# A gated delta-rule attention feeding a GELU layer on one core: the same instructions in another written-out order

## The chip, the core and the metric

The kernel runs on one core of a Trainium2 chip. A core has a matrix engine (TensorE, in the profile PE, with its weight loads as PEld), a vector engine (DVE), a scalar engine (ACT), GpSimd (POOL) and a sync engine (SP) that here only starts transfers. Each engine works through its own queue in order, and semaphores between the engines are the only thing that holds one queue back for another. The metric is the device time of one execution in microseconds (us).

## The reference

Two stages follow each other. The first is a recurrence over 768 steps for each of 4 x 8 heads of width 48, the second a plain two-layer network with a tanh-GELU:

```python
k_n = k / (norm(k) + 1e-6)
for t in range(S):                        # S = 768; state is 48 x 48 for each batch and head
    y[t]  = q[t] @ state
    v_old = state^T @ k_n[t]
    state = state + beta[t] * outer(k_n[t], v[t] - v_old)
x = y.transpose(0, 2, 1, 3).reshape(3072, 384)
h = x @ w_in                              # 384 x 2048
out = gelu_tanh(h) @ w_out                # 2048 x 384
```

## The kernel before, in words

The 768 steps are cut into 12 chunks of 64. Inside a chunk the recurrence becomes products of matrices: the triangular system that couples the 64 steps is inverted by five doubling steps, and only the 48 x 48 state is carried from chunk to chunk. The 32 heads are handled as 2 units of work per chunk (unit u belongs to chunk u // 2), so there are 24 units.

One unit is prepared like this (`prep`). `kc`, `kb` and `qb` bring k, scaled k and q into bf16; `Tc`, `Tb`, `Tk`, `Tq` or `T` transpose them on PE and `kT...` copies the result out of PSUM (from unit 6 on, some transposes are transfers, `turn`). `GM`, `GQ`, `G2` and `G` are the products k k^T and k q^T on PE; `ln`, `wpm`, `wpq` and `wp` copy them out under a triangular mask on DVE (line 527). `X10` and `X11` put the diagonal in (line 557 on POOL, 559 on DVE). Then come the doubling steps i = 1 to 5: a product `A{i}` on PE, `rt{i}` on DVE, which adds twice the identity while it copies out of PSUM (line 580), a product `B{i}` on PE, and a copy back into the block-diagonal operand, `bde{i}0` and `bde{i}1` (line 325, on ACT or DVE) or `bdf` (lines 325 and 331) or `xi` with two `bdc` (line 610). The next step waits for that copy. For a step there are two other forms: `J{i}` and `C{i}` on PE with a plain copy `rj{i}` on ACT or DVE in place of `A{i}` and `rt{i}`; and in the first units `wqa` (a plain copy on ACT) with `wqb` (the mask, on POOL) in place of `wpq`.

`chain` then carries the state over a chunk: `K`, `R`, `U`, `Un`, `S`, `Sn`, `Q`, `O`, `On`, and `X` with `xT`, which hands the chunk to the network. `mlp` is the network: sixteen products `up0` to `up15` on PE (line 717), four `gelu` on ACT (line 721), eight groups `down` on PE (line 728), two copies `Z` and the transfers `out`.

`norms` makes the scale for k: `sq`, `sum`, `pow`, `eps`, `nsq` or `nsa`, `inv`, `ib`. The root of the first three chunks is taken on ACT (`pow` after `tabS`, which loads the table of the root, line 349); `tabG` (line 752) loads the table of the GELU. `warm_up` offers 70 products of zeros, `fill` (line 387), whose result nobody reads; as many of them run as the order names.

The order of all this is written out by hand in a string, `ORDER`: a list of some 1,700 names, each with its engine (`:a` ACT, `:d` DVE, `:g` POOL, `:s` SP; no letter where only one engine is possible) and, for products, its PSUM bank. `Flow.order` puts each name into the queue of its engine in that sequence, and `Flow.emit` adds the semaphore waits that the data and the banks need. Transfers are in the list too: they are issued by SP, ACT or (for the weights) POOL, at the place in that engine's queue where the list names them. q, k and v have three buffers each (chunk modulo 3).

Of the kernel before, what the change touches and what calls it, by code (L numbers as in the profile page):

```python
# [19 lines left out]
betaN000 betaN001 betaN010 betaN011 k1.01:s epsb:d k1.10:a fill45@2 beta11:a k1.11:s fill22@1 beta10:s sq.0b:g tabS pow.0a eps.0a:d twob:d J1.1@3 sum.0b  # L20
q0.1:s mup1 nsa.0a v0.11:s inv.0a ib.0a:d upone0 v0.10:s pow.0b fill55@2 q0.0:a eps.0b:d nsa.0b sq.1:d fill36@0 kb.0:d kc.1:a bdz1:g k2.10:s fill49@2 inv.0b
ib.0b:g kb.1:g betaT1@0 kc.0:a Tc.1@1 fill9@2 betaA111 betaA110 betaA101 sum.1 pow.1 eps.1:g nsq.1:g kTc.1:d q1.1:s fill60@4 Tb.0@2 kTb.0:d Tc.0@4 kTc.0:d
Tb.1@1 inv.1 triwpm0:d betaA100 ib.1:d GM.0@6 ln.0 kb.3:g v1.11:a v0.01:s X11.0:g wpm.0 kTb.1:a GM.1@4 ln.1 X10.0:g v0.00:a qb.0:a Tq.0@1 wpm.1 kc.3:a Tk.3@2
triln3:a A1.0@0 X10.1:d kTq.0:d GQ.0@4 k2.00:a kTk.3:a q1.0:a X11.1:g C1.1 rj1.1:a rt1.0 B1.0@0 k2.01:s pad2:d kb.2:d wpq.0 bde10.0:a kc.2:d GM.3@6 ln.3
B1.1@1 bde10.1:d bde11.0:a A2.0@0 rt2.0 bde11.1:a A2.1@1 rt2.1 Tk.2@3 triwpm2:a B2.0@2 B2.1@0 qb.1:a v1.00:s Tq.1@1 v1.10:s v1.01:s wpm.3 bde21.0:d k2.11:s
sq.2:a sum.2 bde20.0:a A3.0@2 fill1@4 fill4@5 fill42@4 fill14@5 q2.0:s bdf20.1:a bdf21.1:d A3.1@0 rt3.0 B3.0@2 kTk.2:a GM.2@4 rt3.1 triln2:a ln.2 w2.1 qb.2:a
bdz4:g bdz3:g X10.3:g kTq.1:a X11.3:g w1.1 A1.3@0 pad5:g pow.2 B3.1@1 k3.10:s GQ.1@6 wpm.2 rt1.3 kc.5:a k4.10:s q2.1:s bdf30.0:a bdf31.0:a A4.0@2 rt4.0 vs.1:g
B1.3@0 R0b.0:g bdf30.1:a bdf31.1:a A4.1@1 bdz2:g wpq.1 v2.00:s bdf10.3:a qb.3:g eps.2:g B4.0@2 bde41.0:a nsq.2:g bde40.0:a X11.2:g rt4.1 q3.0:s X10.2:g A1.2@4
rt1.2 B4.1@1 bde41.1:d w1.0 bde40.1:a Tq.2@3 kTq.2:d B1.2@4 bde10.2:a triwpm4:g A5.0@5 rt5.0 A5.1@1 rt5.1 bde11.2:a bdf11.3:d k3.01:s B5.0@2 bde50.0:a A2.2@3
rt2.2 B5.1@4 bde50.1:d bde51.0:a k3.00:s bde51.1:a B2.2@0 bde21.2:a bde20.2:a inv.2 A2.3@1 rt2.3 R0a.0:g U.0@4 Un.0:d B2.3@1 A3.2@0 rt3.2 q4.0:s Tq.3@2 O.0@4  # L30
On.0:d fill6@3 bde21.3:a qb.5:g B3.2@0 bde20.3:a A3.3@1 rt3.3 kTq.3:a GQ.3@6 X.0@2 xT.0:d B3.3@1 triwpm5:g bdf30.2:a bdf31.2:a A4.2@0 rt4.2 bdf30.3:a
bdf31.3:d up4.0@2 up12.0@4 up13.0 k3.11:s wpq.3 ib.2:g kb.5:g B4.2@0 up5.0 up6.0 up7.0 up14.0 A4.3@1 up15.0 up0.0@6 q3.1:s tabG bde41.2:d bde40.2:a up1.0
up2.0 A5.2@0 rt4.3 gelu1.0 pad4:g kb.4:g kc.7:a up3.0 B4.3@1 w2.0 kc.4:g sq.3:g sum.3 k4.00:s k5.10:s q4.1:s gelu3.0 gelu0.0 qb.4:g T.4@2 kT.4:a T.5@4 rt5.2
bde41.3:d bde40.3:d kT.5:d pow.3 eps.3:g up8.0@6 up9.0 v2.11:s A5.3@0 rt5.3 k5.00:a G2.5@2 ln.5 bdz5:g kc.6:g X11.5:g k4.01:a G2.4@4 S.0@0 Sn.0:a ln.4 X11.4:g
X10.4:g G.4@2 wp.4 up10.0 qb.9:a up11.0 gelu2.0 nsq.3:g qb.6:g qb.7:g k4.11:s K.1@0 X10.5:g v2.10:s G.5@4 down00.0@2 B5.3@3 wp.5 A1.4@6 bde51.3:a inv.3
down01.0 down10.0@7 k5.11:s rt1.4 v2.01:s q5.0:s v3.01:s ib.3:g k5.01:s R.1 B1.4@6 B5.2@4 down02.0 sq.4:a A1.5@5 down11.0 bdf10.4:a sum.4 GQ.2@0 q5.1:s
bdf50.2:a kb.7:g bdf11.4:a bde50.3:d A2.4@3 q6.0:s bdf51.2:a turn.7 rt1.5 kb.6:g v4.01:a pow.4 eps.4:g B1.5@6 nsq.4:g rt2.4 U.1@4 bde11.5:a qb.11:g kc.9:g
Un.1:a wpq.2 down12.0 B2.4@3 Q.1@0 kc.10:d S.1@4 bde10.5:a bde20.4:d inv.4 O.1 Sn.1 bde21.4:a J2.5@6 On.1:a C2.5 A3.4@3 rt3.4 turn.6 down13.0 rj2.5:a X.1@0
ib.4:d B3.4@5 B2.5@4 qb.8:g sq.5:a xi3.4:a kb.9:g fill27@6 down03.0 xT.1:d bdc30.4:g up0.1@0 sum.5 up1.1 v3.10:a bdc31.4:g up2.1 bdf20.5:a q6.1:s A4.4@5
# [4 lines left out]
nsq.5:g v4.00:a rt2.6 k6.00:s k6.10:s turn.9 R.2 B2.6@6 xi5.5:a bdc50.5:d A2.7@2 kc.11:g bdc51.5:g inv.5 xi2.6:a down00.1@3 gelu3.1 rt2.7 q7.1:a bdc21.6:g
bdc20.6:d U.2@4 B2.7@2 Un.2:a bde21.7:a down12.1 A3.6@6 bde20.7:d Q.2@0 rt3.6 v4.10:s ib.5:g sq.7:g G2.8@4 v3.00:s O.2 ln.8 sq.6:g X11.8:g X10.8:g A3.7@2
down01.1 B3.6@6 S.2@4 sum.7 On.2:a G.8@0 down02.1 rt3.7 Sn.2 bdf30.6:a bdf31.6:a kb.10:g kb.11:g v5.11:s B3.7@2 wp.8 bdf30.7:a A4.6@6 v3.11:s q8.1:a rt4.6
down03.1 bdf31.7:a turnx.2 q7.0:a down13.1 A1.8@0 A4.7@6 turn.10 B4.6@1 G2.9@4 Z0.1:a pow.7 v5.00:s rt1.8 Z1.1:a xi4.6:a v4.11:s G.9@2 bdc41.6:g rt4.7
# [8 lines left out]
A2.10@0 K.4@6 Z1.2:d rt2.10 bdf41.9:a up2.3 up3.3 B1.11@3 v6.01:a G2.12@0 A5.9@2 gelu0.3 R.4 k9.01:a up8.3@6 qb.14:g bde10.11:a bdc50.8:g bde11.11:a v7.00:s
kc.16:g up9.3 B2.10@4 rt5.9 v7.11:a B5.9@5 ln.12 up10.3 inv.7 up4.3@0 bdc51.8:g X11.12:g A2.11@3 xi5.9:d bdc51.9:g bde20.10:a bde21.10:a up5.3 sum.8 out11.2:a
up6.3 up7.3 A3.10@2 rt2.11 up11.3 bdc50.9:g U.4@4 down10.3@3 rt3.10 B2.11@2 gelu1.3 Un.4:d Q.4@0 G2.13@4 gelu2.3 v7.10:s bdf20.11:a G.12@6 O.4 bdf21.11:a
ln.13 down11.3 A3.11@2 On.4:a v6.11:a B3.10@5 G.13@0 wp.12 pow.8 X11.13:g rt3.11 bdf30.10:a eps.8:g S.4@6 down00.3@4 X10.12:g v6.10:a down01.3 bdf31.10:d Sn.4
# [732 lines left out]
```

## Time and profile before

| | |
|---|---|
| time, median of 3 runs | 260.44 us (260.43 to 261.03) |
| the profiled execution | 259.31 us, of which 257.6 us are the span from the first to the last instruction |
| busy in the span | PE 242.8 us (94%), DVE 209.1 us (81%), ACT 185.4 us (72%), POOL 137.7 us (53%) |
| mean granted clock of PE | 0.98 |
| transfers | 31.46 MB in 116,788 packets, mean 122 GB/s |

Busy times are those of the profiled execution. A transfer that an engine issues is not counted as busy time of that engine; such rows carry a q behind the engine's name (SPq, ACTq, POOLq), and their duration is the time that issuing took. In a row of the timeline the first number is the start in us, the second the duration; what stands in brackets at its end is the time that the engine sat idle before it and what it waited for. Durations of PE are modelled and overlap, so that eight products can show 0.6 us and the next eight start after 0.3 us.

### The profile page before, as it was taken

What the parts mean: (1) busy time and instruction counts of PE and PEld (TensorE: products, weight loads), DVE (VectorE), ACT (ScalarE), POOL (GpSimd) and SP (SyncE); (2) the same over time, 40 slices, a digit from 0 to 9 for tenths busy, and PEclk for the clock granted to TensorE, in tenths of its full rate; (3) what the DMA queues carried; (4) which work ended last, traced back from release to release, by engine and by line L of the source; (5) the groups of instructions that cost most, each with busy time, mean ns of one, the idle gap of its engine ahead of it and who ended that gap; (6) DMA issues with size and microseconds to landing.
All of it is one profiled execution on the core that took longest, in us unless ns stands there. A gap on an engine that the chain in (4) does not pass through costs nothing.

```text
span 257.6 us, 12254 instructions
## 1 busy us (share of the span) xinstructions
PE 242.8 (94%) x5491; PEld 190.4 (74%) x5491; DVE 209.1 (81%) x363; ACT 185.4 (72%) x295; POOL 137.7 (53%) x206
## 2 busy tenths in 40 slices
PE   7878789999999989999999999999999999999994
PEld 2466569677877868977877887778877878878772
DVE  6898998999989779999999899789887889575000
ACT  0679989688978868966967876977856766665252
POOL 4488666995989918763576786536370330240000
PEclk9965999999999999999999999999999999999999
DMA  5999999999968965948959359247867031011322
GB/s 90 199 193 195 202 193 191 167 198 128 173 122 171 191 103 98 147 98 157 185 109 193 67 114 181 45 93 110 147 96 142 3 64 36 30 36 33 64 61 61
DMA packets 116788, 31.46 MB, mean 122 GB/s; under 512 B 110848, under 2 KB 115968, under 8 KB 116736
## 3 DMA queue, kind: packets, MB, share of 16 engines
q1 hardware_dynamic: 84448, 19.82, 46.9%
q10 hardware_dynamic: 29408, 7.72, 16.1%
q0 software_dynamic: 2880, 3.15, 7.6%
q8 instruction: 43, 0.70, 1.1%
q14 instruction: 9, 0.07, 0.1%
HBM read 20.64 MB, written 4.72 MB: 98 GB/s over the span
## 4 chain that ended last, share of the span: by engine, by line
PE 82%; DVE 12%; ACTq 2%; ACT 2%; issue 1%
PE ps L728 24%; PE ps L717 24%; PE ps L568 21%; PE ps L523 4%; PE ps L640 3%; DVE bd L325 2%; DVE rt L580 2%; PE ps L663 2%; DVE wp L527 2%; ACTq L425 2%; DVE ln L527 2%; PE ps L688 1%; PE ps L675 1%; DVE kT L325 1%; PE ps L387 1%
## 5 line engine op out<-in xcount | busy, mean ns | idle before, releaser
L717 PE MATMUL ps<-xT,W 128*128 128x256 bf16 x576 | 77.6, 273 | 0.0
L325 ACT ACTIVATE bd<-ps 64x512 bf16<-64x512 f32 x110 | 62.8, 588 | 19.2 <-PE ps L568 17.8
L728 PE MATMUL ps<-W,gT 128*128 128x384 bf16 x384 | 74.2, 326 | 0.0
L721 ACT ACTIVATE gT<-ps 128x1024 bf16<-128x1024 f32 x48 | 48.8, 1020 | 19.1 <-PE ps L717 18.1
L717 PEld LDWEIGHTS ps<-xT,W 128*128 128x128 bf16 x576 | 50.5, 98 | 6.8
L580 DVE TENSOR_TENSOR rt<-ps,two 128x512 bf16<-128x512 f32 x70 | 47.2, 683 | 6.6 <-PE ps L568 6.0
L728 PEld LDWEIGHTS ps<-W,gT 128*128 128x128 bf16 x384 | 33.2, 98 | 16.6 <-ACT gT L721 0.2
L610 POOL COPY bd<-xi 64x256 f32<-64x256 f32 x45 | 19.3, 429 | 46.9 <-ACT xi L325 25.7
L557 POOL TENSOR_SCALAR_AFFINE_SELECT bd<-ln 64x512 bf16<-64x512 bf16 x42 | 28.3, 674 | 14.9 <-DVE ln L527 10.2
L527 DVE CAST_PREDICATED wp<-mup,ps 128x1024 bf16<-128x1024 uint16 (+1 forms) x28 | 29.7, 1065 | 1.4 <-PE ps L523 1.1
L568 PE MATMUL ps<-rt,bd 128*128 128x64 bf16 x576 | 28.5, 196 | 1.5 <-DVE rt L580 1.5
L568 PE MATMUL ps<-wp,bd 128*128 128x64 bf16 (+1 forms) x576 | 28.3, 190 | 1.7 <-DVE ob L325 0.6
L568 PEld LDWEIGHTS ps<-wp,bd 128*128 128x128 bf16 x576 | 23.4, 99 | 6.7 <-DVE ob L325 1.0
L568 PEld LDWEIGHTS ps<-rt,bd 128*128 128x128 bf16 x576 | 23.8, 100 | 5.8 <-DVE rt L580 2.3
L451 POOL TENSOR_TENSOR nrm<-nrm,half 128x16 f32<-128x16 f32 x9 | 26.2, 2908 | 3.2 <-DVE nrm L449 3.0
L580 DVE TENSOR_TENSOR rl<-ps,two 128x384 bf16<-128x384 f32 (+1 forms) x48 | 23.0, 484 | 4.7 <-PE ps L568 4.1
L325 DVE CAST bd<-ps 64x512 bf16<-64x512 f32 x35 | 23.8, 686 | 2.9 <-PE ps L568 2.2
L568 PE MATMUL ps<-ln,bd 128*128 128x48 bf16 (+1 forms) x384 | 18.8, 190 | 2.4 <-issue 1.1
L331 ACT ACTIVATE bd<-ps,up 128x512 bf16<-128x512 f32 x30 | 20.1, 675 | 0.9 <-DVE bd L325 0.7
L568 PE MATMUL ps<-rl,bd 128*128 128x64 bf16 x384 | 19.1, 193 | 0.8 <-DVE rl L580 0.8
L568 PEld LDWEIGHTS ps<-ln,bd 128*128 128x128 bf16 x384 | 15.9, 98 | 5.1 <-ACT bd L325 1.3
L478 POOL TENSOR_TENSOR tok<-kraw,nrm 128x384 bf16<-128x384 f32 x19 | 15.7, 835 | 6.1 <-DVE nrm L460 2.8
(101 smaller groups left out, 341.4 us busy)
## 6 DMA issues: line engine op xcount, KB each, us to landing
qraw<-in_q_dram SPq DMA_DIRECT2D x16, 192.0 KB, 5.4
vraw<-in_v_dram SPq DMA_DIRECT2D x31, 96.0 KB, 4.2
kraw<-in_k_dram SPq DMA_DIRECT2D x28, 96.0 KB, 4.3
out_dram<-ob ACTq DMA_DIRECT2D x12, 192.0 KB, 3.6
out_dram<-ob SPq DMA_DIRECT2D x10, 192.0 KB, 2.8
vraw<-in_v_dram ACTq DMA_DIRECT2D x17, 96.0 KB, 3.6
kraw<-in_k_dram ACTq DMA_DIRECT2D x16, 96.0 KB, 3.8
qraw<-in_q_dram ACTq DMA_DIRECT2D x8, 192.0 KB, 4.3
```

The source lines that it names most:

```text
L325: return e.activation(out, in_, ACT.Copy) if e is nc.scalar else e.tensor_copy(out, in_)
L331: return e.activation(out, in_, ACT.Copy, scale=up1[:, 0:1]) if e is nc.scalar else e.tensor_scalar(out, in_, up1[:, 0:1], None, op0=ALU.mult)
L451: if e is nc.scalar else e.tensor_tensor(nr[:, 1, hx], nr[:, 0, hx], half[:, hx], ALU.pow), reads=[nrn, "half"] + ["one", "roots"] * (c < ...
L478: A(("dve", "pool"), op("kb"), lambda e, P: e.tensor_tensor(kb, kr, nr[:, 5, hx].unsqueeze(2).to_broadcast(full), ALU.mult), reads=[f"kraw ...
L527: return e.copy_predicated(out.rearrange("p (x g) t -> p x g t", x=2), mask[:, 0:wd].bitcast(U16).unsqueeze(1).unsqueeze(1).to_broadcast([ ...
L557: A(("pool", "dve"), op(f"X1{a}"), lambda e, P, src=ln[m][hf(a), :, :], dst=bd[b_][hf(a), :, hf(a)], a=a: e.affine_select(out=dst, in_=src ...
L568: ins = e.matmul(P(name)[:, C * h + cs.start:C * h + cs.stop], bd[b_][:, h, :], rhs[:, h, cs], **kw)
L580: A(("dve",), op(f"rt{i}"), lambda e, P, i=i, cs=cs, cn=cn, r_=r_: e.tensor_tensor(r_[:, :, cs], P(ps(f"A{i}")).rearrange("p (h t) -> p h ...
L610: A(("pool", "dve"), op(f"bdc{i}{a}"), lambda e, P, src=xi[i_][hf(a), :, :], dst=bd[b_][hf(a), :, hf(a)]: e.tensor_copy(dst.bitcast(F32), ...
L717: ins = e.matmul(P(ph)[:, 256 * f:256 * f + 256].rearrange("p (x t) -> p x t", x=2), W1[:, j, 128 * (i + f):128 * (i + f) + 128], x_[:, :, ...
L721: A(("act",), f"gelu{i // 4}.{c}", lambda e, P, i=i, ph=ph: e.activation(g_[:, i:i + 4, :], P(ph).rearrange("p (f t) -> p f t", f=4), ACT. ...
L728: ins = e.matmul(P(po)[:, 0:DM], g_[:, f, 128 * b:128 * b + 128], W2[:, f, :], start=(f == 0), stop=(f == FC - 1))
```

## The change

Every one of the names in `ORDER` gets a new place, and many a new engine or a new form. What the program computes is the same. 1,722 names become 1,727. Counted over the whole string:

- `fill`: 31 products of zeros become 37. Up to the first `up`, 28 become 36; behind it, 3 become 1.
- The form `wqa` and `wqb` replaces `wpq` in units 0, 1 and 2. `J1` and `C1` with `rj1` replace `A1` and `rt1` in unit 0, and `A2` with `rt2` replaces `J2`, `C2` and `rj2` in unit 5.
- Instructions that change engine, for example: `ladj16` and `two` from DVE to ACT, `kTc.0` and `kTc.1` from DVE to ACT, `kc` of 7 more units onto POOL, `vs` of 2 chunks from DVE to POOL, 4 of the `Z` from ACT to DVE.
- Transfers of q, k and v issued by ACT: 46 become 52, with more of them early. Among the first 54 transfers of the old list the sequence among each other is kept; `v2.01` and `v2.10`, which came behind them, now stand in between.

The diff replaces the whole string. Of its 88 lines, three of the new ones that hold places spoken of below:

```diff
@@ ORDER @@
...
+ORDER = """upone0 wz:d bdz2:d tmplz:d tmpl0 fill14@5 mmup:d epsb:d beta01:a tmpl1 pad1:d ident:g fill36@4 pad0:d triwpm3:g half:g triwpm0:d k0x1.11:a ladj16:a fill52@7
...
+B2.1@5 kTq.1:a bde20.0:a A3.0@1 wqb.0 bde20.1:d bde21.1:a GM.2@2 GQ.1@4 rt3.0 fill23@0 A3.1@7 w1.1 qb.3:g B3.0@0 wqa.1 k3.10:a ln.2 fill37@1 X10.3:g sq.2:g
...
+up15.0 B4.2@3 kTq.2:d up4.0@4 up5.0 qb.5:g bdf31.3:a up6.0 A4.3@2 up7.0 kb.4:g bdf40.2:a up0.0@6 sq.3:d qb.4:g gelu3.0 sum.3 k4.00:s up2.0
...
```

(A `+` line of the string is a line of the new list; all lines of the old one go. Because the new string is one line longer, every line number below it is one higher in the changed kernel: 325 becomes 326, 580 becomes 581.)

Three places, row by row. The first is the start of ACT's queue, before and then after. In these rows `braw` is beta, `kraw` is k as loaded, `one` the operand of the table load `tabS`, `rl_0<-tmpl` is `ladj16`, and the first `nrm<-nrm 128x8` is `pow.0a`.

```order
L393 DMA braw<-in_beta_dram 32x64
L425 DMA kraw<-in_k_dram 64x4x48 x5
L425 DMA kraw<-in_k_dram 64x8x48
L393 DMA braw<-in_beta_dram 32x11x64
L349 ACT_TABLE_LOAD
L349 ACTIVATE one<-one 128x1
L450 ACTIVATE nrm<-nrm 128x8
L457 ACTIVATE nrm<-nrm,epsb 128x8
L450 ACTIVATE nrm<-nrm 128x8
```

```order
L394 DMA braw<-in_beta_dram 32x64
L426 DMA kraw<-in_k_dram 64x4x48
L378 ACT_TABLE_LOAD
L378 ACTIVATE rl_0<-tmpl 128x32x16
L426 DMA kraw<-in_k_dram 64x4x48 x4
L350 ACT_TABLE_LOAD
L350 ACTIVATE one<-one 128x1
L426 DMA kraw<-in_k_dram 64x8x48
L394 DMA braw<-in_beta_dram 32x11x64
L451 ACTIVATE nrm<-nrm 128x8
```

`ladj16` now stands behind the second transfer and brings a table load of its own; the load for the root comes after four more transfers, and two transfers come behind that.

The second place is DVE's queue in the second doubling step of units 0 and 1. `rt<-ps,two` is `rt`, `bd<-ps` is `bde`, `bd<-ps,up` is half of `bdf`, `ln` and `wp` under line 527 (528) are the masked copies, `nrm<-sq` is `sum.2`, and `tok` is `kb`, `kc` or `qb`. Before:

```order
L527 COPY_PREDICATED wp<-mup,ps 128x8x64
L325 CAST tok<-kraw 128x8x48
L527 COPY_PREDICATED ln<-mlo,ps 128x512
L325 CAST bd<-ps 64x8x64
L580 TENSOR_TENSOR rt<-ps,two 128x512 x2
L527 COPY_PREDICATED wp<-mup,ps 128x8x64
L325 CAST bd<-ps 64x8x64
L449 TENSOR_REDUCE nrm<-sq 128x16
L331 TENSOR_SCALAR bd<-ps,up 128x8x64
L580 TENSOR_TENSOR rt<-ps,two 128x512 x2
```

After:

```order
L326 CAST tok<-qraw 128x8x48
L326 COPY wp<-tmpl 128x1024
L367 MEMSET tok 128x24x8
L528 COPY_PREDICATED ln<-mlo,ps 128x512
L528 COPY_PREDICATED wp<-mup,ps 128x8x64
L326 CAST bd<-ps 64x8x64
L581 TENSOR_TENSOR rt<-ps,two 128x512 x2
L326 CAST bd<-ps 64x8x64 x2
L581 TENSOR_TENSOR rt<-ps,two 128x512
L528 COPY_PREDICATED ln<-mlo,ps 128x512
```

Between `rt2.1` and `rt3.0` there stood a masked copy, a copy, the sum of chunk 2 and a scaled copy; now there are two copies.

The third place is ACT's queue over the first two doubling steps. `wp<-ps` is `wqa`, `rt<-ps` is `rj1`, `vraw` and `qraw` are v and q as loaded. Before:

```order
L325 ACTIVATE rt<-ps 128x512
L325 ACTIVATE bd<-ps 64x8x64 x3
L325 ACTIVATE wp<-tmpl 128x1024
L325 ACTIVATE tok<-qraw 128x8x48
L447 ACTIVATE sq<-kraw 128x768
L325 ACTIVATE bd<-ps 64x8x64 x2
L325 ACTIVATE kT<-ps 128x1024
L325 ACTIVATE ln<-tmpl 128x512
```

After:

```order
L326 ACTIVATE rt<-ps 128x512
L326 ACTIVATE bd<-ps 64x8x64 x3
L426 DMA vraw<-in_v_dram 64x8x48
L326 ACTIVATE kT<-ps 128x1024
L426 DMA vraw<-in_v_dram 64x8x48
L326 ACTIVATE kT<-ps 128x512
L326 ACTIVATE bd<-ps 64x8x64 x2
L326 ACTIVATE wp<-ps 128x8x64
L426 DMA kraw<-in_k_dram 64x8x48
L326 ACTIVATE bd<-ps 64x8x64
L426 DMA kraw<-in_k_dram 64x8x48
```

The preset of `wp`, the copy of q, the square of chunk 2 and the preset of `ln` are gone from here; transfers of v and k, which SP issued or which came later, stand between the copies.

More of the change, by code (lines that the diff above doesn't have):

```diff
@@ L20 @@
[L20 to L39, printed above, removed]
@@ L44 @@
[L44 to L47, printed above, removed]
@@ L56 @@
[L56 to L59, printed above, removed]
```

147 lines of the change are left out of this document (87 added, 60 removed).

## The prediction, written before the changed kernel ran

> **What bounds the kernel now.** I read the page first, then the busy time by stage, then who waited for whom, then the timeline of the start. The page says that PE is the busiest engine, and its slices say where it is not:
>
> ```profile
> span 257.6 us, 12254 instructions
> PE 242.8 (94%) x5491; PEld 190.4 (74%) x5491; DVE 209.1 (81%) x363; ACT 185.4 (72%) x295; POOL 137.7 (53%) x206
> ...
> PE   7878789999999989999999999999999999999994
> ...
> DVE  6898998999989779999999899789887889575000
> ...
> PEclk9965999999999999999999999999999999999999
> ```
>
> The view by stage, cut where the first `up` starts (38.6) and where PE ends (254.2), columns as its heading names them:
>
> ```profile
> core 0: us, PE busy (x) PEld busy (x) DVE busy (x) ACT busy (x) POOL busy (x), PEclk, DMA share, GB/s
> 0.00:13.00 13.00, 10.01 (x96) 4.72 (x100) 9.87 (x42) 4.90 (x14) 5.78 (x19) 1.00 0.88 145
> 13.00:26.00 13.00, 10.81 (x212) 8.27 (x212) 12.15 (x21) 10.73 (x20) 10.92 (x17) 0.61 1.36 194
> 26.00:38.60 12.60, 9.70 (x303) 7.97 (x296) 12.44 (x22) 11.23 (x22) 8.22 (x14) 1.00 1.13 197
> 38.60:50.00 11.40, 11.05 (x263) 9.48 (x262) 10.44 (x15) 9.37 (x13) 8.40 (x11) 1.00 1.21 187
> 50.00:254.20 204.20, 201.28 (x4654) 159.92 (x4650) 164.17 (x265) 148.74 (x230) 104.43 (x147) 1.00 0.62 108
> 254.20:257.60 3.40, 0.00 (x0) 0.00 (x0) 0.00 (x0) 0.45 (x1) 0.00 (x0) 1.00 0.43 116
> ```
>
> The reader is to see two stages. From 38.6 to 254.2 us PE is busy for 212.3 of 215.6 us; it bounds there, and nothing on another engine counts unless it makes PE wait. Before 38.6 PE is busy less, though 28 products of zeros are counted in. From 13.0 to 38.6 DVE is busy for 24.6 of 25.6 us and ACT for 22.0, where ACT's transfers aren't counted. That stretch is a chain over the first two units, product, `rt` on DVE, product, copies on ACT or DVE, and it ends with `xT.0`, which lets the first `up` go:
>
> ```profile
> 13.01 0.69 DVE L527 CAST_PREDICATED ln<-mlo,ps 128x512 bf16<-128x512 uint16 x1
> ...
> 38.02 0.56 DVE L325 COPY xT<-ps 128x768 bf16<-128x768 bf16 x1
> ...
> 38.63 0.61 PE L717 MATMUL ps<-xT,W 128*128 128x256 bf16 x4
> ```
>
> So the time is: the moment at which `xT.0` is ready, plus the work that PE then still has (212.3), plus what PE waits on the way (215.6 - 212.3 = 3.3, of which the largest are below), plus 3.4 for the last copy and its transfers.
>
> ```profile
> PE ps L568 <- issue: 1.1, 1, 1.1
> PE ps L568 <- DVE ob L325: 0.6, 1, 0.6
> PE ps L523 <- DVE wp L527: 0.5, 1, 0.5
> ```
>
> **The change part by part.** All sums are against the profiled execution: 259.31 us, the span of 257.6 and 1.7 around it. The median of the runs is 260.44, so I carry the difference over to that.
>
> *The start, up to `ln.0` at 13.0: 0.* ACT gets one more table load. These rows price it and show what it holds up:
>
> ```profile
> 6.00 1.28 ACT L349 ACT_TABLE_LOAD   x1 [6.00 <-issue]
> 7.29 0.20 ACT L349 ACTIVATE one<-one 128x1 f32<-128x1 f32 x1
> 7.53 0.21 ACT L450 ACTIVATE nrm<-nrm 128x8 f32<-128x8 f32 x1
> ...
> 13.32 0.52 ACT L325 ACTIVATE tok<-qraw 128x384 bf16<-128x384 f32 x1 [0.48 <-DMA qraw<-in_q_dram]
> 13.33 0.60 ACTq L425 DMA_DIRECT2D kraw<-in_k_dram  x1
> 13.75 0.51 ACT L325 ACTIVATE tok<-kraw 128x384 bf16<-128x384 f32 x1
> 14.16 0.61 ACT L325 ACTIVATE ln<-tmpl 128x512 bf16<-128x512 bf16 x1
> ```
>
> The load takes 1.28 us of the engine. The transfer at 13.33 stands in the queue behind the copies that begin at 13.75 and 14.16, and is issued before they begin: the sequencer runs ahead of the engine, and only a semaphore wait holds it. So the transfers behind `ladj16` wait for what `ladj16` waits for, the second half of `tmpl` on POOL (about 2.6 us by my walk through the queue), and not for the load. The third transfer of k goes from about 2.0 to 2.6 us, `sq.0a` moves some 0.6 us; `pow.0a`, today held to 7.53 by the table load at 6.00, can go at about 7.0, since that load now stands behind six transfers and not eight. Behind it the norms stand differently: `kb.0` comes 0.8 us later, the transposed copy of `kc` is out of the way by then, and `GM.0` comes out where it is. I take 0 for `ln.0`; from -0.5, if POOL is quicker than I walked, to +1.3, if the load does hold the transfers.
>
> The Trainium skill, page "ScalarE: Activation LUTs", section "What ACT_TABLE_LOAD costs", speaks against the change: it gives 1283 ns for the load and about 1380 ns more for a drain, some 2.66 us for each switch. The load agrees to the nanosecond (mean 1283 in the groups); the drain doesn't show here, as 7.29 follows 6.00 + 1.28 at once. By that page this part would be up to +2.7.
>
> *From `ln.0` to `xT.0`: -1.4.* DVE's work there, grouped in the stretch from 13.0 to 38.6:
>
> ```profile
> L580 DVE TENSOR_TENSOR rt<-ps,two 128x512 bf16<-128x512 f32 x11 | 7.5, 686 | 0.7 <-PE ps L568 0.7
> L527 DVE CAST_PREDICATED wp<-mup,ps 128x512 bf16<-128x512 uint16 x6 | 4.1, 682 | 0.0
> L325 DVE CAST bd<-ps 64x512 bf16<-64x512 f32 x4 | 2.7, 684 | 0.1
> L331 DVE TENSOR_SCALAR bd<-ps,up 128x512 bf16<-128x512 f32 x2 | 1.5, 748 | 0.0
> L325 DVE COPY kT<-ps 128x512 bf16<-128x512 bf16 x2 | 0.8, 418 | 0.0
> L325 DVE CAST tok<-kraw 128x384 bf16<-128x384 f32 x1 | 0.7, 723 | 0.0
> ...
> L559 DVE TENSOR_TENSOR bd<-ln,twob 64x512 bf16<-64x512 bf16 x1 | 0.4, 410 | 0.0
> ```
>
> Between these two ends the new list takes from DVE one `rt` (0.69), two `wpq` (1.36), one scaled copy (0.75), two `kT` (0.84) and `kc.2` (0.72), 4.36 us. It adds one `bde` (0.68), one diagonal (0.41), `qb.1` (0.72 as for `kc.2`), a preset of `wp` and a few norms (about 0.6, an estimate from 0.4 for copies of that kind): 2.4 us. Net -1.9, were DVE the only bound. It isn't: `rj1.0` and the two `wqa` go to ACT, at 0.59 each as its copies; from ACT go the presets, the square and two copies of q there (the third place above), so ACT has about 2 us less too, and its transfers cost the sequencer 0.60 each while the engine works. The masks `wqb` go to POOL, 0.84 to 1.47 (its other products of 384 and 768 columns), and nothing reads them before `O.0`, some 10 us later. What shortens the way most is that `sum.2` and `wpm.3` no longer stand between `rt2.1` and `rt3.0`. Later, where `A4.0` stands behind `B1.3` on PE, part of it is given back. Walking the queues with these durations I get `xT.0` at 36.4 to 37.4 in place of 38.02, and take -1.4; bounds -1.9 and 0.
>
> *PE's work behind the first `up`: -0.5.* Two products of zeros fewer and one product with the identity (`J2.5`) less; a product of 512 columns costs 0.2 to 0.39 us there. The eight more ahead of it lie where PE waits: it is idle for 13.00 - 10.01 and for 12.60 - 9.70 us in two of the three early stages.
>
> *Waits of PE behind the first `up`: 0.* They are 3.3 us now. DVE loses about 7 us of work over the whole run and ACT gains 5 and the load, both counted by the same prices, so DVE is less pressed and ACT a little more; in the new list ten `B` stand within 1 us of PE work behind their `A`, in the old one six, and such a `B` waits if its `rt` is late. I see no net direction: 1.8 to 6.5 us, that is -1.5 to +3.2. The 1.1 us that the profile calls issue has no cause that I can move.
>
> *The end: 0.* The last copy and two transfers stand as before, one on each queue.
>
> Sum: 0 - 1.4 - 0.5 + 0 + 0 = -1.9, so 257.4 for a profiled execution and **258.5** for the median.
>
> **The rivals.**
>
> *ACT's transfers hold up its copies (slower).* From the third place on ACT issues seven transfers between about 16 and 33 us, where today it issues none. SP issues them now, and its rows there look like this:
>
> ```profile
> 20.59 5.73 SPq L425 DMA_DIRECT2D vraw<-in_v_dram  x1
> 26.36 0.64 SPq L416 DMA_DIRECT2D qraw<-in_q_dram  x1
> 27.04 5.41 SPq L425 DMA_DIRECT2D kraw<-in_k_dram  x2
> ...
> 33.32 2.96 SPq L425 DMA_DIRECT2D kraw<-in_k_dram  x1
> ```
>
> A transfer that takes 0.60 to issue elsewhere takes up to 5.73, as if its queue were full. If that happens to ACT, every copy behind it waits. Two of 2.96 cost 4.7 beyond the usual, -1.9 + 4.7 = +2.8: 263.2. It decides from 1.9 us of such holding on. Against it: at most five of ACT's transfers would be under way at once (4 us to landing), while SP had eight or more when it first stalled.
>
> *The square of chunk 3 holds up DVE (no change).* `sq.3` goes from POOL to DVE, ahead of `rt4.3`, for which `B4.3` and all of PE behind it wait. Today it waits for its data:
>
> ```profile
> 40.15 1.46 POOL L448 TENSOR_TENSOR sq<-kraw 128x768 f32<-128x768 f32 x1 [2.14 <-DMA kraw<-in_k_dram]
> ```
>
> If k of chunk 3 lands at 40.15 again, `sq.3`, `sum.3` (0.95 each) and `rt4.3` (0.5) end at 42.5, and PE, with ups until about 41, stands for 1.5 us: 260.0. For the forecast k must land by 38.7; it should, for five fewer transfers of SP stand ahead of its last quarter, and one of the four goes by ACT.
>
> The Trainium skill, page "DMA: Bandwidth & Descriptors", section "Issuing engines are not separate DMA queues", says that a second issuing engine saves only the time of issuing, not the transfer's. By that k lands no earlier, and this rival holds.
>
> *PE waits more behind the first `up` (slower).* The tighter `B` wait and ACT is late with `gelu`: 3.3 becomes 6.4, and the gain of 1.9 turns into +1.2: 261.6. For it speaks that DVE is busy 164 of 204 us and everything changes place; against it, that no wait there exceeds 1.1 now.
>
> *The clock stays up (faster still).* The granted clock is 0.61 in the stage from 13 to 26. If the eight more products of zeros keep it at 1.00, about six products on the chain take 0.4 in place of 0.6: -1.2 more, 257.3.
>
> **How the numbers follow.** Chances: forecast 0.45, ACT held up 0.15, DVE held up by `sq.3` 0.12, more waits 0.15, clock 0.08, the start late by 1.3 (259.8, no change) 0.05. A measurement of this kernel can't tell less than 0.3% (0.8 us) from no change. Faster than 259.7: 0.44 of the forecast and the clock, 0.52. Slower than 261.2: 0.30. The rest 0.18. The range reaches from the clock's case with a wait less (255.8) to just short of ACT held up twice (262.6); the forecast's own is 257.0 to 260.0.
>
> **What would show it.** Right: `ln.0` near 13, `xT.0` at 36.4 to 37.4, the first `up` behind it, PE busy about 212 from there, ACTq rows of 0.6 throughout. Wrong: ACTq rows over 1 us between 16 and 33; an idle DVE ahead of line 449 near 39; `ln.0` past 14; PE idle over 5 us behind the first `up`.

## The result and the profile after

The change is faster, by little: 259.18 us (median of 18 runs, 257.3 to 260.84) against 260.88 for the kernel before (18 runs beside it), ratio **0.9943, 95% interval 0.992 to 0.9966**. The forecast was 258.5 us, in a range of 255.8 to 262.6. A second chip later gave 0.9907 (0.9871 to 0.9944).

The profiled execution of the change took 259.73 us, 0.4 us *more* than that of the kernel before (259.31). That is no contradiction: executions of one kernel differ by some us here, and the first profile of before lies near the lower end of its runs (257.83 to 266.06), while the change's runs lie close together. So a place where the two profiles differ by 1 us proves nothing by itself; the table below has more profiles of both kernels. The profiles of e1_before, e12_before and e10_late_sqlate are of executions over 1.5% above the fastest of their kernel, and such executions are left out of the ratios.

From the page of the changed kernel, the lines that answer to those of before:

```profile
span 258.0 us, 12268 instructions
PE 241.1 (93%) x5490; PEld 189.0 (73%) x5497; DVE 206.2 (80%) x354; ACT 191.1 (74%) x305; POOL 140.8 (55%) x205
...
PEclk9999979999999999999999999999999999999999
```

And its busy time by stage, cut where its own first `up` starts (39.10) and where PE ends (254.46); the columns are those of the same view before (busy us and count of PE, PEld, DVE, ACT, POOL, then clock, DMA share, GB/s):

```profile
0.00:13.00 13.00, 9.93 (x83) 4.50 (x84) 10.39 (x36) 7.70 (x17) 7.82 (x28) 1.00 0.89 137
13.00:26.00 13.00, 9.96 (x263) 7.16 (x267) 11.64 (x22) 10.19 (x20) 11.52 (x15) 1.00 1.40 192
26.00:39.10 13.10, 9.67 (x243) 8.04 (x243) 11.42 (x21) 10.41 (x21) 10.81 (x17) 0.87 1.20 208
39.10:50.00 10.90, 10.65 (x234) 8.89 (x230) 9.99 (x17) 10.19 (x14) 6.58 (x9) 1.00 1.29 200
50.00:254.46 204.46, 200.88 (x4682) 160.45 (x4678) 162.75 (x262) 152.10 (x236) 104.09 (x138) 1.00 0.63 107
254.46:258.00 3.54, 0.00 (x1) 0.00 (x0) 0.00 (x0) 0.49 (x1) 0.00 (x0) 0.89 0.43 111
```

The granted clock stays at 1.00 from 13 to 26, where it was 0.61 before, and gives up some in the next stage. DVE, busy 24.6 of 25.6 us there before, is now busy 23.1 of 26.1. Yet the chain ends no earlier in this execution. The three ends that the prediction named, from the timeline:

```profile
13.11 0.69 DVE L528 CAST_PREDICATED ln<-mlo,ps 128x512 bf16<-128x512 uint16 x1
...
38.49 0.56 DVE L326 COPY xT<-ps 128x768 bf16<-128x768 bf16 x1
...
39.10 1.16 PE L718 MATMUL ps<-xT,W 128*128 128x256 bf16 x9
```

`ln.0` is where it was, `xT.0` came at 38.49 and not at 36.4 to 37.4. ACT's queue in the stretch between shows what may have been in the way (its transfers, and the copy that stands behind the longest):

```profile
24.60 1.08 ACTq L426 DMA_DIRECT2D kraw<-in_k_dram  x1
...
27.02 2.34 ACTq L417 DMA_DIRECT2D qraw<-in_q_dram  x1
27.39 1.07 ACT L326 ACTIVATE bd<-ps 64x512 bf16<-64x512 f32 x2
29.40 0.59 ACT L326 ACTIVATE bd<-ps 64x512 bf16<-64x512 f32 x1 [0.94 <-PE ps L569]
...
34.35 1.02 ACTq L417 DMA_DIRECT2D qraw<-in_q_dram  x1
```

The issue of `q3.0` takes ACT's sequencer until 29.36, and the copy behind it starts at 29.40. The profile puts that idle time down to PE, the semaphore that came last by its reckoning; the end of the issue fits better, and e4_sp and e5_late tested it.

All profiles side by side (us; the medians are of all runs, the ratios are to the kernel before, measured beside it on the same chip):

| kernel | median | ratio, 95% | profiled | `xT.0` | square of chunk 3 starts | first `up` to PE's end |
|---|---|---|---|---|---|---|
| before | 260.44 | 1 | 259.31 | 38.02 | 40.15 | 215.5 |
| e1_before | 261.87 | 0.9992 (0.9949 to 1.0035) | 265.03 | 39.65 | 44.06 | 219.6 |
| e12_before | 261.98 | 1.0013 (0.9976 to 1.005) | 264.78 | 37.78 | 45.64 | 221.2 |
| the change | 259.18 | 0.9943 (0.992 to 0.9966) | 259.73 | 38.49 | 40.68 | 215.4 |
| e8_after | 258.79 | 0.9907 (0.9871 to 0.9944) | 258.69 | 38.21 | 42.02 | 214.6 |
| e7_ladj | 259.16 | 0.9914 (0.9879 to 0.9949) | 258.49 | 38.97 | 41.16 | 213.7 |
| e6_nofill | 259.86 | 0.9927 (0.9893 to 0.9962) | 260.57 | 39.11 | 41.73 | 215.2 |
| e2_newhead | 261.49 | 1.0025 (0.9993 to 1.0057) | 263.01 | 38.64 | 39.44 | 217.8 |
| e3_oldhead | 262.81 | 1.0061 (1.0029 to 1.0094) | 264.89 | 39.38 | 45.46 | 218.2 |
| e4_sp | 264.23 | 1.0123 (1.0088 to 1.0158) | 265.41 | 37.08 | 46.02 | 222.4 |
| e5_late | 261.28 | 0.9988 (0.995 to 1.0025) | 262.23 | 37.53 | 42.88 | 218.8 |
| e9_sp_sqlate | 263.35 | 1.0086 (1.0048 to 1.0124) | 263.73 | 37.58 | 46.35 | 220.3 |
| e10_late_sqlate | 261.80 | 1.0018 (0.9984 to 1.0051) | 263.83 | 36.10 | 42.58 | 221.9 |
| e11_after_sqlate | 261.63 | 1.0035 (0.9997 to 1.0072) | 261.62 | 37.38 | 38.25 | 218.4 |

e1 to e4 ran on one chip, e5 to e8 on a second, e9 to e12 on a third.

The start of the square is the landing of k of chunk 3 only where its row shows a wait for the transfer. In the change DVE had other work until 40.68: by the trace the last of the four quarters, `k3.10`, issued by ACT at 23.82, landed 15.6 us later, at 39.4. In e8_after the last one landed at 42.0, as the square started.

### The profile page after: what moved, and what is told of

Same layout as the page of the kernel before. It is cut to its first block, busy times and chain, and to the rows that moved or that the text cites. A ratio compares the mean times of both kernels' runs of the same rounds, so it can differ in the third digit from the quotient of the medians.

```text
span 258.0 us, 12268 instructions
## 1 busy us (share of the span) xinstructions
PE 241.1 (93%) x5490; PEld 189.0 (73%) x5497; DVE 206.2 (80%) x354; ACT 191.1 (74%) x305; POOL 140.8 (55%) x205
## 4 chain that ended last, share of the span: by engine, by line
PE 78%; DMA 6%; POOL 4%; ACT 4%; SPq 2%; DVE 2%; issue 2%; ACTq 1%; POOLq 0%
PE ps L729 24%; PE ps L718 23%; PE ps L569 20%; DMA kraw<-in_k_dram 3%; PE ps L524 3%; PE ps L641 3%; DMA qraw<-in_q_dram 2%; SPq L426 2%; PE ps L664 2%; PE ps L689 1%; PE ps L676 1%; ACT bd L326 1%; DVE rt L581 1%; POOL bd L558 1%; ACTq L426 1%
## 5 line engine op out<-in xcount | busy, mean ns | idle before, releaser
L326 ACT ACTIVATE bd<-ps 64x512 bf16<-64x512 f32 x122 | 70.6, 589 | 27.9 <-PE ps L569 26.0
L722 ACT ACTIVATE gT<-ps 128x1024 bf16<-128x1024 f32 x48 | 48.0, 1019 | 14.9 <-PE ps L718 14.2
L558 POOL TENSOR_SCALAR_AFFINE_SELECT bd<-ln 64x512 bf16<-64x512 bf16 x40 | 26.6, 669 | 21.5 <-DVE ln L528 18.8
L611 POOL COPY bd<-xi 64x256 f32<-64x256 f32 x36 | 14.8, 415 | 34.7 <-ACT xi L326 26.9
L569 PE MATMUL ps<-wp,bd 128*128 128x64 bf16 (+1 forms) x576 | 27.0, 188 | 1.9 <-ACT bd L332 0.6
L528 DVE CAST_PREDICATED wp<-mup,ps 128x1024 bf16<-128x1024 uint16 (+1 forms) x25 | 27.6, 1107 | 0.5 <-PE ps L524 0.4
L479 POOL TENSOR_TENSOR tok<-kraw,nrm 128x384 bf16<-128x384 f32 x21 | 17.6, 840 | 8.9 <-PE ps L676 8.4
L569 PE MATMUL ps<-ln,bd 128*128 128x64 bf16 (+1 forms) x384 | 18.7, 190 | 0.9 <-ACT bd L326 0.6
L528 DVE CAST_PREDICATED ln<-mlo,ps 128x512 bf16<-128x512 uint16 x24 | 16.4, 682 | 3.6 <-PE ps L524 3.3
```

The lines of the kernel that those rows point to most:

```text
L326: return e.activation(out, in_, ACT.Copy) if e is nc.scalar else e.tensor_copy(out, in_)
L479: A(("dve", "pool"), op("kb"), lambda e, P: e.tensor_tensor(kb, kr, nr[:, 5, hx].unsqueeze(2).to_broadcast(full), ALU.mult), reads=[f"kraw ...
L528: return e.copy_predicated(out.rearrange("p (x g) t -> p x g t", x=2), mask[:, 0:wd].bitcast(U16).unsqueeze(1).unsqueeze(1).to_broadcast([ ...
L558: A(("pool", "dve"), op(f"X1{a}"), lambda e, P, src=ln[m][hf(a), :, :], dst=bd[b_][hf(a), :, hf(a)], a=a: e.affine_select(out=dst, in_=src ...
L569: ins = e.matmul(P(name)[:, C * h + cs.start:C * h + cs.stop], bd[b_][:, h, :], rhs[:, h, cs], **kw)
L611: A(("pool", "dve"), op(f"bdc{i}{a}"), lambda e, P, src=xi[i_][hf(a), :, :], dst=bd[b_][hf(a), :, hf(a)]: e.tensor_copy(dst.bitcast(F32), ...
```

## The experiments

All of them are edits of `ORDER` alone. In the diffs a `-` or `+` line is a piece of the string, not all of it. Their line numbers are one or two lower than the change's, since the string is broken into lines differently.

### Theories

The prediction put the gain ahead of the first `up` (-1.4 of -1.9). First theory: the gain is there, and ACT's transfers take part of it back. Rival: the gain lies behind the first `up`, in when k of chunk 3 lands and how the rest is ordered around it.

### e1_before and e12_before: the kernel before, again

No edit.

> The kernel before once more, only to see how far one execution of it differs from another: ratio 1.000 within 0.2%. The theory that the gain sits ahead of the first up, because PE is cold there for about 10 us in the kernel before and for about 4 in the changed one, expects a mean granted clock of about 0.98 in its runs and the first up between 38.5 and 40 us in this profile; the theory that the gain sits behind the first up expects the first up at 38.6 again and more waits of PE behind it than the 3.3 us of the profile already seen (4.5 or more).

> The kernel before once more, ratio 0.997 to 1.003. Asked of its profile: where xT.0 lies in an ordinary execution. If the first profile was a quick one, xT.0 is at 38.8 to 39.6 here, and most of the change's gain lies ahead of the first up; if it is at 38.0 again, the gain lies behind it, and the time from the first up to PE's end is above 216.

Ratios 0.9992 and 1.0013, both with 1 inside their intervals of about 0.37% to either side. e12's `xT.0` came at 37.78, earlier than in the first profile: the expectation that an ordinary execution of the old head is later than 38.02 is not borne out there (e1 had 39.65), though at 265.03 and 264.78 us neither profile is of an ordinary execution. What e12 lost, it lost behind that. Its timeline, SP's issue of the last quarter of k of chunk 3 (by its place in the list), POOL's square of it, and the next product that waited:

```profile
34.72 3.16 SPq L424 DMA_DIRECT2D kraw<-in_k_dram  x1
...
45.64 1.46 POOL L447 TENSOR_TENSOR sq<-kraw 128x768 f32<-128x768 f32 x1 [7.86 <-DMA kraw<-in_k_dram]
...
47.61 2.74 PE L486 MATMUL ps<-ident,tok 128*128 128x128 bf16 x24 [4.24 <-POOL tok L324]
```

The transfer was issued 1.4 us later than in the first profile (33.32 there) and landed 5.5 us later (40.15). POOL stood for 7.86 us, the copy of q behind the square was late, and PE stood for 4.24 us. In this execution the late transfer cost PE most of its delay.

### e2_newhead and e3_oldhead: one part of the change without the other

e2_newhead has the change's list up to the first `up`, then the old one; e3_oldhead the other way round. At the seam, the change and then e2:

```diff
-bdf30.3:a tabG q3.1:s rt4.2 wpq.3 up12.0@0 w2.0 ib.2:g up13.0 up14.0 up15.0 B4.2@3 kTq.2:d
+tabG q3.1:s rt4.2 wpq.3 kTq.2:d triwpm4:g qb.5:g bdf31.3:d up4.0@2 up12.0@4 up13.0 ib.2:g kb.5:g
```

At the seam, the kernel before and then e3:

```diff
-A4.2@0 rt4.2 bdf30.3:a bdf31.3:d up4.0@2 up12.0@4 up13.0 k3.11:s wpq.3 ib.2:g kb.5:g B4.2@0
+v2.01:a v2.10:a bdz5:g k3.11:s kc.4:d tabG q3.1:s wpq.3 up12.0@0 w2.0 ib.2:g up13.0 up14.0 up15.0 B4.2@3
```

> The new list up to its first up, then the old list for all that is left. If the gain of 0.57% sits ahead of the first up: ratio to before 0.994, span about 256.5. If it sits behind the first up: 1.000 to 1.003 (xT.0 was 0.5 us later in the one profile of the change, 38.49 against 38.02).

> The old list up to its first up, then the new list for all that is left. If the gain sits ahead of the first up: ratio to before 1.000. If it sits behind the first up: 0.994 or less (0.992).

Neither half carries the gain: 1.0025 and 1.0061. For e3 a row of DVE shows one reason, the square of chunk 3 that now stands in DVE's queue while the old head's transfers bring k late:

```profile
45.46 0.96 DVE L447 TENSOR_TENSOR sq<-kraw 128x768 f32<-128x768 f32 x1 [2.96 <-DMA kraw<-in_k_dram]
...
PE ps L567 <- DVE rl L579: 2.4, 1, 2.4
```

DVE stands for 2.96 us, and the list of who waited (the lower row: us in total, times, longest) shows PE standing 2.4 us for what is queued behind the square. In e2 k landed early (39.44) and no single wait explains the 217.8 us behind its first `up`, so what the old rest loses behind the new head stays open. Both lists also have a joint that neither kernel has: the first `up` starts 1.4 us behind `xT.0` in e2 (40.04) and 2.0 in e3 (41.36), against 0.6 in the change. With these 0.8 and 1.4 us taken off, an estimate from one profile each, the ratios would be about 0.999 and 1.001, still no gain. So the first theory in its plain form, 0.994 for e2, falls; how much of the loss belongs to the joints is not shown.

### e4_sp: the early transfers back on SP

```diff
-v2.01:a
-v2.10:a
-k3.10:a
-k4.10:a
-q3.0:a
-q4.0:a
+v2.01:s
+v2.10:s
+k3.10:s
+k4.10:s
+q3.0:s
+q4.0:s
```

(Each at its own place in the list.)

> The changed kernel with v2.01, v2.10, k3.10, k4.10, q3.0 and q4.0 issued by SP at the same places of the list, so that ACT issues no transfer between k2.00 and the first up. If ACT's transfers that took 1.08 and 2.34 us to issue held up its copies: xT.0 about 1 us earlier than 38.49 (37.5) and ratio to before about 0.990. If what held the chain was something else: xT.0 at 38.5 and 0.994. If k of chunk 3 then lands late and sq.3 on DVE waits for it: an idle DVE of 1 us or more ahead of sq.3, and 0.997 to 1.000.

Two things came out at once. The timeline and the list of PE's waits:

```profile
33.79 6.04 SPq L424 DMA_DIRECT2D kraw<-in_k_dram  x1
...
37.08 0.56 DVE L324 COPY xT<-ps 128x768 bf16<-128x768 bf16 x1
...
46.02 0.96 DVE L447 TENSOR_TENSOR sq<-kraw 128x768 f32<-128x768 f32 x1 [6.67 <-DMA kraw<-in_k_dram]
...
PE ps L567 <- DVE rl L579: 6.2, 1, 6.2
```

`xT.0` came at 37.08, inside the forecast's 36.4 to 37.4: without transfers on ACT the walk through the queues was right. But SP comes to the last quarter of k of chunk 3 only at 33.79 and takes 6.04 us to issue it, k lands at 46.0 in place of 39.4 or 42.0 in the change's two profiles, DVE stands 6.67 us ahead of `sq.3`, and PE 6.2. The ratio is 1.0123. So in these profiles ACT's transfers cost about 1.1 to 1.4 us at `xT.0`, and they save more than that behind it.

### e5_late: three of them moved, later

```diff
-k4.10:a
-q3.0:a
-q4.0:a
-k3.11:s A3.3@6
+k3.11:s q3.0:s k4.10:s q4.0:s A3.3@6
```

> The changed kernel with only k4.10, q3.0 and q4.0 taken from ACT; SP issues them directly behind k3.11, so that nothing stands ahead of k of chunk 3 that did not stand there in the changed kernel. If the two faces of the transfers are all there is to it (ACT's copies held up by k4.10 and q3.0; DVE's sq.3 waiting for k of chunk 3): xT.0 at 37.0 to 37.6 as without ACT's transfers (37.08), sq.3 with no idle ahead of it, span about 256.5, ratio to before 0.988 to 0.991. If ACT's hold-up was not what moved xT.0: 38.5 and 0.994. If q of chunk 3 or k of chunk 4 now land too late: xT.0 at 37.3, but PE idle by more than the 3.6 us of the changed kernel's profile behind the first up, and 0.994 or more.

The three issues that held ACT are gone from the early part, and `xT.0` comes at 37.53, as expected. k lands at 42.9, little later than in e8_after (42.0), and DVE, there sooner, waits longer for it:

```profile
37.53 0.56 DVE L324 COPY xT<-ps 128x768 bf16<-128x768 bf16 x1
...
42.88 0.96 DVE L447 TENSOR_TENSOR sq<-kraw 128x768 f32<-128x768 f32 x1 [3.07 <-DMA kraw<-in_k_dram]
...
PE ps L567 <- DVE rl L579: 2.5, 2, 2.3
PE ps L522 <- issue: 1.4, 2, 1.1
PE ps L567 <- issue: 1.2, 1, 1.2
PE ps L687 <- issue: 1.1, 1, 1.1
```

Up to one us won ahead of the first `up`, 2.3 lost at the square (1.26 in e8_after), and three waits that the profile calls issue, of 1.1 to 1.2 us, which I cannot assign. Ratio 0.9988: the gain of the change is gone.

### e6_nofill: the products of zeros

```diff
-fill3@1
-fill45@2
-fill6@2
-fill26@6
-fill27@6
-fill12@0
-fill23@0
-fill37@1
-fill8@5
-fill49@1
-fill47@4
-fill56@1
```

> The changed kernel without the twelve products of zeros that stand between the first copy of k and xT.0 (fill3, 45, 6, 26, 27, 12, 23, 37, 8, 49, 47, 56); nobody reads their result. If they make the gain by keeping the clock up: mean granted clock 0.98 or less (the kernel before has 0.981 over 34 runs, the changed one 0.991 over 18) and ratio to before 0.998 to 1.002. If the chain ahead of the first up hangs on DVE and ACT and not on PE's clock: clock lower all the same, ratio 0.993 to 0.995.

From the view by stage, the stretch from 13 to 26 us and that from 26 to its first `up`:

```profile
13.00:26.00 13.00, 9.19 (x294) 7.08 (x282) 11.99 (x24) 11.29 (x23) 11.80 (x15) 1.00 1.37 188
26.00:40.12 14.12, 12.14 (x238) 10.75 (x235) 11.52 (x20) 9.87 (x19) 10.39 (x16) 0.50 1.19 213
```

The clock drops to 0.50 for the whole of the second stretch (0.87 with them), and `xT.0` comes at 39.11, 0.6 to 0.9 us later than in the change's two profiles. The ratio, 0.9927, is 0.002 above that of e8_after, measured on the same chip, and the intervals overlap. The clock of that stretch is worth some tenths of a per cent at most. From 13 to 26 it stays at 1.00 without them, so what the rise from 0.61 there is worth is not shown.

### e7_ladj: without the extra table load

```diff
-ladj16:a
+ladj16:d
```

> The changed kernel with ladj16 on DVE again, so that ACT's extra table load is gone. If the load is hidden, as forecast: ln.0 at 13.1 as before it, ratio to before 0.994 as the changed kernel. If the load and what it holds up cost their 1.3 us: ln.0 at 12 to 12.5 and 0.990.

Ratio 0.9914 against 0.9907 of e8_after; `ln.0` at 12.90. The table load costs nothing that can be measured.

### e8_after: the change again

No edit.

> The changed kernel once more, for a second profile and on the chip of the three above: ratio to before 0.994 within 0.25%, xT.0 between 38.2 and 39, no idle ahead of sq.3, an ACTq row of over 1 us for q3.0. The theory that the gain sits partly behind the first up expects 215 to 216 us from the first up to PE's end (215.4 in the first profile), the kernel before 215.5 to 219.6.

Ratio 0.9907. Its rows show the same hold of ACT and a small stall at the square (ACT, DVE, PE):

```profile
26.45 2.46 ACTq L415 DMA_DIRECT2D qraw<-in_q_dram  x1
...
42.02 0.96 DVE L447 TENSOR_TENSOR sq<-kraw 128x768 f32<-128x768 f32 x1 [1.53 <-DMA kraw<-in_k_dram]
...
44.48 0.41 PE L567 MATMUL ps<-rl,bd 128*128 128x64 bf16 x8 [1.26 <-DVE rl L579]
```

Here DVE waits for k, and PE stands 1.26 us. So in this execution the change is still held up by that transfer; in its first profile it was not.

### e9, e10 and e11: the square of chunk 3 later

If DVE's wait ahead of `sq.3` is the loss in e4 and e5, the square should go to POOL and its sum further back. The same edit on e4 (e9_sp_sqlate), on e5 (e10_late_sqlate) and on the change itself (e11_after_sqlate):

```diff
-bdf40.2:a up0.0@6 sq.3:d qb.4:g gelu3.0 sum.3 up1.0
+bdf40.2:a up0.0@6 qb.4:g gelu3.0 up1.0
...
-rt4.3 kb.5:g B4.3@2
+rt4.3 kb.5:g sq.3:g B4.3@2
...
-T.4@4 gelu0.0 pow.3 A5.2@2
+T.4@4 gelu0.0 A5.2@2
...
-rt5.2 rt5.3 q4.1:a S.0@2 eps.3:g
+rt5.2 rt5.3 sum.3 pow.3 eps.3:g q4.1:a S.0@2
```

> The change with the six early transfers back on SP (as in e4_sp), and with the square of chunk 3 on POOL behind kb.5 and its sum and root on DVE only behind rt5.3. If DVE's wait of 6.7 us ahead of sq.3 was all that e4_sp lost: xT.0 at 37.0 to 37.5, no wait of PE above 1.5 us at 40 to 50, and the gain at xT.0 (1.1 to 1.4 us against the change) kept, ratio to the kernel before about 0.985 to 0.990, less than the change's 0.991. If k of chunk 3 at 46 is late for its other readers too (POOL's copies of k behind the square, the scale for k, K.1): the wait moves there, PE stands 2 to 5 us between 46 and 60, ratio 1.00 to 1.01.

> The same later place of the square of chunk 3, with the transfers of e5_late (only k4.10, q3.0 and q4.0 moved to SP, behind k3.11, so that k of chunk 3 lands near 42 to 43). First theory: xT.0 at 37.5, PE's wait of 2.3 us is gone, ratio 0.987 to 0.992 (e5_late had 0.9988). Second: ratio stays at 0.996 to 1.000.

> The change with the later place of the square of chunk 3 alone; ACT keeps its transfers, so xT.0 stays at 38.2 to 38.5. If DVE's wait there still costs the change something (PE waited 1.3 us once in one of its two profiles): ratio 0.987 to 0.990. If that wait has slack: 0.990 to 0.992, as the change.

The times of the first theory came in none of the three: 1.0086, 1.0018 and 1.0035. e9 and e10 can't be told from e4 and e5 (the intervals overlap). In e9 DVE's wait ahead of the square is gone. PE's two largest waits from 38 to 62 us, and a wait of ACT between them:

```profile
42.04 0.39 PE L716 MATMUL ps<-xT,W 128*128 128x256 bf16 x2 [2.58 <-issue]
...
53.86 0.31 ACT L456 ACTIVATE nrm<-nrm,epsb 128x16 f32<-128x16 f32 x1 [2.55 <-POOL nrm L452]
...
55.13 0.41 PE L567 MATMUL ps<-rl,bd 128*128 128x64 bf16 x8 [1.46 <-ACT gT L720]
```

The first ends at 42.04, before k lands at 46.3, so it is not the wait for k that the second theory had; the profile names no releaser. The other two are what the edit itself brings, for e11 has them too, with k early. e10 has them as well (2.55 for ACT, 2.71 for PE). So e9 and e10 leave open whether DVE's wait is what e4 and e5 lose: the edit takes that wait away and adds one of its own.

e11 was outside what either theory had: it loses all of the change's gain, though in its profile `xT.0` came early (37.38) and k of chunk 3 earlier than in any other (38.25). A stretch of e11, on POOL, DVE, ACT and PE, and its busy time from 50 to 60:

```profile
38.25 1.47 POOL L447 TENSOR_TENSOR sq<-kraw 128x768 f32<-128x768 f32 x1 [0.74 <-DMA kraw<-in_k_dram]
...
45.90 0.94 DVE L448 TENSOR_REDUCE nrm<-sq 128x16 f32<-128x768 f32 x1
...
46.92 2.94 POOL L450 TENSOR_TENSOR nrm<-nrm,half 128x16 f32<-128x16 f32 x1 [1.79 <-DVE nrm L448]
...
50.19 0.31 ACT L456 ACTIVATE nrm<-nrm,epsb 128x16 f32<-128x16 f32 x1 [2.55 <-POOL nrm L452]
50.41 1.00 ACT L720 ACTIVATE gT<-ps 128x1024 bf16<-128x1024 f32 x1
...
51.47 0.41 PE L567 MATMUL ps<-rl,bd 128*128 128x64 bf16 x8 [1.46 <-ACT gT L720]
...
50.00:60.00 10.00, 7.82 (x149) 5.31 (x152) 6.58 (x9) 7.22 (x12) 9.27 (x13) 0.83 0.77 125
```

The same in e8_after, which is the change:

```profile
43.01 0.95 DVE L448 TENSOR_REDUCE nrm<-sq 128x16 f32<-128x768 f32 x1
...
49.11 0.30 ACT L456 ACTIVATE nrm<-nrm,epsb 128x16 f32<-128x16 f32 x1
49.55 1.02 ACT L720 ACTIVATE gT<-ps 128x1024 bf16<-128x1024 f32 x1
...
50.00:60.00 10.00, 9.77 (x280) 7.43 (x279) 9.12 (x14) 9.04 (x16) 9.69 (x11) 1.00 1.00 168
```

The square is data for a chain of its own: sum on DVE, root on POOL (2.94 us), `nsa.3` on ACT, which stands in ACT's queue ahead of a `gelu`. With the sum at 45.90 ACT stands 2.55 us for that chain, the `gelu` behind it is late, PE waits 1.46 us for it, and is busy 7.82 of 10 us from 50 to 60, against 9.77. With the sum at 43.01 there is no such wait. The square itself was done earlier in e11 (39.72) than in e8_after (42.98); what came late is the sum, which the edit put behind `rt5.3`, and with it the root. So an early sum and root of chunk 3, which the prediction counted only as work that delays DVE, are among the things that the change needs: they make the scale for k of chunk 3 in time. That the square has to be on DVE for it is not shown. PE waits 5.9 us behind the first `up` in e11 and 3.0 in e8_after; this chain is 1.46 of the difference, and the rest is open. No version came out that beats the change.

## Why the prediction was right, and where it was not

The total was right (-1.9 us forecast; -1.5 by the ratio, -1.7 by the medians of all runs), the split was not, and that they agree is in part luck. The profiled spans of the change are 258.0 and 257.0 us (e8_after) against 257.6, so +0.4 and -0.6, and the term that was to bring most of the gain did not come.

*The start: 0.* Right, for the reason given. ACT's rows:

```profile
1.98 1.28 ACT L378 ACT_TABLE_LOAD   x1 [1.98 <-issue]
2.73 0.64 ACTq L426 DMA_DIRECT2D kraw<-in_k_dram  x1
3.27 0.63 ACT L378 ACTIVATE rl<-tmpl 128x512 bf16<-128x512 bf16 x1
...
5.41 1.28 ACT L350 ACT_TABLE_LOAD   x1 [1.51 <-issue]
...
7.14 0.21 ACT L451 ACTIVATE nrm<-nrm 128x8 f32<-128x8 f32 x1 [0.24 <-DVE nrm L450]
```

A transfer is issued at 2.73, while the load of 1.98 runs; `pow.0a` goes at 7.14 (walked: 7.0; before: 7.53); `ln.0` moved by 0.1. e7_ladj takes the load away and gains nothing. The Trainium skill, page "ScalarE: Activation LUTs", section "What ACT_TABLE_LOAD costs", would have had up to 2.7 us here; the copy at 3.27 follows 1.98 + 1.28 at once, so these rows show the load and no drain.

*From `ln.0` to `xT.0`: -1.4.* This is the step that failed. The walk (36.4 to 37.4) was about right for ACT's copies alone: `xT.0` is at 37.08 and 37.58 in e4 and e9, where all six transfers are on SP, and at 37.53 and 36.10 in e5 and e10, where three are. In the change it was 38.49 and 38.21, since the sentence "its transfers cost the sequencer 0.60 each while the engine works" doesn't hold for `q3.0`: 2.34 and 2.46 us. No semaphore wait stands in these rows, so the premise that only such a wait holds the sequencer was too narrow: issuing itself held it. Two more took 1.0 in the first profile. Beyond 0.60 each these are 2.6 us, of which 1.0 to 1.4 reached `xT.0` in these profiles (38.49 against 37.53 and 37.08). In e11, where that issue took 0.80, `xT.0` was at 37.38 with the same list. So the rival of ACT held up did happen, at under a third of its price (4.7), and the reason that I gave against it, the small number of ACT's transfers under way, was no protection. Against the old head the step is worth less still: its four profiles (the first, e1, e3, e12) have 37.78 to 39.65, mean 38.7; the five with the new head, its fills and its transfers on ACT (the change, e2, e7, e8, e11) have 37.38 to 38.97, mean 38.3. That is -0.4, less than either scatters.

*PE's work: -0.5.* About right: 10.65 + 200.88 = 211.5 us busy from the first `up`, against 212.3, so -0.8.

*Waits of PE behind the first `up`: 0.* Inside its bounds: 3.8 us in the change (215.4 - 211.5), 3.0 in e8 and 2.3 in e7, against 3.3 in the first profile of before, so -1.0 to +0.5. DVE lost 2.9 us of work over the whole run (209.1 to 206.2) and not 7; ACT gained 5.7, about as counted. Whether the gain of the medians lies in this term is not shown. In e1 and e12 these waits are 5.0 and 6.7 us, with k of chunk 3 landing at 44.0 and 45.6, but these executions took 265.03 and 264.78 us, far above the old kernel's median, and can't stand for it. I took the 3.3 of one profile for a property of the kernel; it belonged to an execution in which k landed at 40.1.

*The end: 0.* Right, 3.54 us against 3.4.

*The square of chunk 3 holds up DVE.* It did not decide, but not for my reason. I had said that k must land by 38.7, and that it should, since fewer transfers of SP stand ahead of its last quarter. SP's issue of that quarter in the change:

```profile
22.26 2.25 SPq L426 DMA_DIRECT2D kraw<-in_k_dram  x1
```

It is 11 us earlier than before (33.32), and this quarter landed at 33.8. But the quarter that ACT issues landed at 39.4, so k as a whole came hardly earlier than before (40.1). DVE had work until 40.68, and nothing was lost; in e8 k landed at 42.0 and PE lost 1.26. The Trainium skill, page "DMA: Bandwidth & Descriptors", section "Issuing engines are not separate DMA queues", says that a second issuing engine saves the time of issuing alone; I took from it that k lands no earlier. The trace agrees with the page and not with what I drew from it: SP's last quarter took 11.5 and 16.1 us from issue to landing with ACT's share (the change and e8) and 12.2 with SP alone (e4), so no transfer became quicker. But SP begins to issue it at 33.79 with SP alone, and at 22.26 and 25.90 with ACT's share, and the landing of k moves with it, from 46.0 to 39.4 and 42.0. The times differ by 1.8 to 2.2% (1.0123 against 0.9943 and 0.9907).

*The clock.* It did stay up from 13 to 26, as that rival had it, and fell for part of the next stage. e6 puts the worth of the clock in that next stage at a few tenths of a per cent at most; what the stage from 13 to 26 gained by it was not tried.

**What stays open.** Where the gain of the medians lies is not shown. The three profiles of before are of executions of 259.3, 264.8 and 265.0 us, and none is from the middle of the old kernel's spread (its runs: 257.8 to 266.1 us; the 30 runs of the change: 257.3 to 261.0). Shown is which parts the gain needs: the transfers on ACT (e4, e5), an early sum and root of chunk 3 (e11), and, as far as the joints let one say, both halves of the list (e2, e3). How much each contributes against the kernel before is not shown, since taking one away loses more than the whole gain. The waits called issue, up to three of 1.1 us or more in a profile, have no cause that I found.

## What to carry to other kernels

A single profile of a kernel whose runs spread by 3% may show an uncommon execution: before a stretch of it is taken as the base of a sum, take a second one, and compare where each transfer landed. Don't count 0.6 us for every issue of a transfer: here one issue took up to 2.46 us on ACT in the change and 6.04 on SP in e4, and on a compute engine it held the next copy; taking the transfers away from there cost more, since the other engine then came late to a transfer that others waited for. And an instruction that looks like mere bookkeeping, such as the sum of a square on the busiest vector engine, may stand in a chain that another engine's queue waits for: follow it to its last reader before moving it.
